# Eight more weight slices decoded by halves, two more chunks turned on VectorE, and a new order for the first 360 steps

## The chip, the cores and the metric

The kernel runs on one core of one Trainium2 chip. The metric is device time in microseconds of one execution. Engines are named as in the profile: PE is TensorE (PEld its weight loads), DVE is VectorE, ACT is ScalarE, POOL is GpSimd, SP is SyncE, which only issues transfers here. A transfer is called a DMA.

## The reference

A gated linear attention recurrence, whose output is the input of a two-layer block with a hard-swish between.

```python
# q, k, v, alpha: (batch 4, heads 8, seq 768, dim 48), float32
state = zeros(B, H, D, D)
for t in range(S):
    state = alpha[:, :, t, :, None] * state + einsum('bhd,bhe->bhde', k[:, :, t], v[:, :, t])
    y[:, :, t] = einsum('bhd,bhde->bhe', q[:, :, t], state)
x = y.transpose(0, 2, 1, 3).reshape(3072, 384)
h = x @ w_in                               # (384, 2048), arrives as float64
g = h * clip(h + 3, 0, 6) / 6
out = g @ w_out                            # (2048, 384), arrives as float64
```

## The kernel before

**Attention.** The 768 positions of each of the four sequences are cut into six chunks of 128, so there are 24 chunks, numbered 0 to 23. For a chunk, alpha, k and q have to stand with the head dimension along the partitions. There are two ways to get there. Chunks below `FIRST` are loaded token by token into a ring of three buffers, one DMA for each of a, k and q, and `transposed` turns each by four 128x128 transposes on PE (line 283) into a PSUM bank; ACT copies alpha out of that bank (`place_alpha`, line 312), and the two products of `scaled` (line 341) read PSUM. Chunks from `FIRST` on are loaded by four DMAs of 32 partitions each for a, k and q (line 264) into `quads`, of which there are two sets used in turn, and DVE turns each by one 32x32-block transpose (line 287 for alpha, line 291 for k and q); `scaled` then reads SBUF (line 343), and POOL clears four columns of the place that alpha was in (line 347). Two running products along the tokens (`decay` line 321, `growth` line 333) give the factors by which k and q are scaled. PE computes scores in two halves of 64 tokens (line 360), the outputs (line 470) and the update of the state (line 444). ACT places q and the state beside scores and v (lines 380 and 433), and copies the finished chunk of x out of PSUM (`keep_x`, line 479) and, for chunks below 8, the turned-back k (`keep_k`, line 392).

**Weights.** The weights come as float64 and are decoded on the chip. They are cut into 16 slices of 128x768 values, 768 KB each, 0 to 7 of `w_in` and 8 to 15 of `w_out`, loaded through five raw buffers (line 161 and line 165). A slice is decoded in five or fewer steps:

- `d1`, `round_low` (ACT, line 185): the low words are scaled and rounded.
- `dx`, `sign` (ACT, line 190): the upper 16 bits of the rounded low words are set from the sign, only for slices in `BY_HALVES`.
- `d2`, `magnitude` (ACT, line 195): the absolute value of the high words.
- `d3`, `high_bits` (DVE): for slices in `BY_HALVES` a clip and a shift (lines 202 and 204), for the others a clip, a shift with a mask, and a third operation that joins the sign (lines 206, 207, 209).
- `d4`, `add_low` (POOL, line 216): the sum of both words as integers.

Before the change slices 0, 1, 2 and 4 go by halves.

**The two layers.** Group g is a pair of chunks. Groups 0 and 1 are done plainly (`ff1` lines 493 and 504, the gate lines 509 and 513, `ff2` line 531). From group 2 on the first layer is done by products of sums of blocks (`product1`, line 617, with sums on DVE), and from group 1 on the second (`product`, line 720).

**Order.** The order is written out by hand as one long string of steps, such as `d3.9` or `tq.4.0`, which are run one after another; each engine does its own instructions in that order, and waits on semaphores for the others. In the string `la`, `lk`, `lq`, `lv` and `w` are loads, and they stand in one queue of SP. `ta`, `tk`, `tq` turn, `ca` is `place_alpha`, `r` and `p` are the running products, `k` and `q` the scalings, `sc`, `u`, `ya`, `yb` the matmuls of the attention, `cy` is `keep_x`. `z.m.n` is filler: matmuls of the identity on n blocks of 128 columns, whose result nobody reads (line 548); 48 of the 49 blocks stand near the start.

## Time and profile before

| | |
|---|---|
| median of 3 runs | 531.0 us (530.9 to 531.11) |
| profiled execution, its own time | 530.91 us |
| its span | 529.1 us |
| mean granted TensorE clock | 0.999 |
| instructions | 15082 |
| DMA bytes read from HBM | 44.50 MB |

The span is what the views of the profile divide; 1.8 us of the profiled execution's time lie outside it. Busy time of an engine is the time in which at least one of its instructions runs. In the strip of 40 slices one slice is 13.2 us. A wait is shown with who ended it.

### The profile page before, as it was taken

Reading aid. Unit: us, or ns where it says so; the run is one execution under the profiler, and the core shown is the slowest. Engines: PE = TensorE matmul, PEld = TensorE weight load, DVE = VectorE, ACT = ScalarE, POOL = GpSimd, SP = SyncE. Lnnn points to the kernel's source line nnn. Section 1 sums busy time; section 2 is a strip of 40 time slices with the busy share of each in tenths; the row PEclk is TensorE's granted clock in tenths of the full one; section 3 lists DMA queues with packets and bytes.
Section 4 is the critical chain, followed back from the end, with each engine's and each line's share of the span. In section 5 each row is a group of like instructions: output and inputs, shape, how many; then the busy total and the mean of one; then the engine's idle time right before and its main releaser. Section 6 shows DMA issues by size and latency. Waiting matters only on the chain.

```text
span 529.1 us, 15082 instructions
## 1 busy us (share of the span) xinstructions
PE 520.6 (98%) x6290; PEld 494.8 (94%) x6290; DVE 462.0 (87%) x838; ACT 259.6 (49%) x513; POOL 55.3 (10%) x89
## 2 busy tenths in 40 slices
PE   8799999999999999999999999999999999999997
PEld 6598886789999999999999999999999999999997
DVE  6998999999999999999999999899988896395471
ACT  4968875112755453464365355454353552543330
POOL 5333543100000100101000000000000000000000
PEclk9999999999999999999999999999999999999999
DMA  9998794213245365445452546153330214000001
GB/s 180 253 240 261 181 269 117 54 32 93 58 118 118 92 135 135 104 95 150 82 145 63 110 118 160 41 124 79 108 84 25 61 22 100 17 26 7 9 9 37
DMA packets 124100, 54.40 MB, mean 103 GB/s; under 512 B 83328, under 2 KB 116864, under 8 KB 124032
## 3 DMA queue, kind: packets, MB, share of 16 engines
q1 hardware_dynamic: 124032, 53.44, 42.8%
q8 instruction: 49, 0.80, 0.7%
q14 instruction: 19, 0.16, 0.1%
HBM read 44.50 MB, written 8.91 MB: 101 GB/s over the span
## 4 chain that ended last, share of the span: by engine, by line
PE 90%; DVE 4%; SPq 2%; DMA 2%; ACT 1%; issue 1%; POOL 0%; DVEq 0%; POOLq 0%; ACTq 0%
PE m_ps L720 36%; PE m_ps L617 31%; PE m_ps L493 6%; PE m_ps L531 4%; PE t_ps L470 4%; PE t_ps L360 2%; PE m_ps L504 2%; PE m_ps L548 2%; PE t_ps L444 1%; PE t_ps L283 1%; DMA rings<-in_alpha_dram 1%; DVE g_sb L554 1%; SPq L253 1%; PE t_ps L388 1%; SPq L410 0%
## 5 line engine op out<-in xcount | busy, mean ns | idle before, releaser
L720 PE MATMUL m_ps<-w,g_sb 128*128 128x192 f32 x704 | 121.8, 327 | 0.0
L623 ACT COPY g_sb<-m_ps 128x512 f32<-128x512 f32 x110 | 63.5, 583 | 116.6 <-PE m_ps L617 91.6
L720 PEld LDWEIGHTS m_ps<-w,g_sb 128*128 128x128 f32 x704 | 113.8, 190 | 0.5
L720 PE MATMUL m_ps<-rings,g_sb 128*128 128x192 f32 x528 | 91.3, 326 | 0.0
L720 PEld LDWEIGHTS m_ps<-rings,g_sb 128*128 128x128 f32 x528 | 85.4, 190 | 0.3
L617 PE MATMUL m_ps<-xc,w 128*128 128x128 f32 x640 | 82.1, 276 | 0.3 <-ACT g_sb L623 0.3
L617 PEld LDWEIGHTS m_ps<-xc,w 128*128 128x128 f32 x640 | 77.7, 192 | 1.2 <-ACT g_sb L623 0.4
L509 ACT ACTIVATE r<-g_sb,half 128x512 f32<-128x512 f32 x80 | 56.8, 721 | 36.3 <-DVE g_sb L558 17.5
L513 DVE SCALAR_TENSOR_TENSOR g_sb<-r,g_sb 128x512 f32<-128x512 f32 x80 | 53.8, 684 | 9.1 <-ACT r L509 8.7
L617 PE MATMUL m_ps<-xT,raw 128*128 128x128 f32 x400 | 53.2, 278 | 0.0
L617 PEld LDWEIGHTS m_ps<-xT,raw 128*128 128x128 f32 x400 | 48.8, 192 | 0.7 <-ACT g_sb L623 0.2
L664 DVE TENSOR_TENSOR g_sb<-g_sb 128x512 f32<-128x512 f32 (+1 forms) x55 | 42.2, 796 | 4.8 <-PE m_ps L720 4.5
L617 PE MATMUL m_ps<-xT,w 128*128 128x128 f32 x320 | 41.8, 277 | 0.0
L617 PEld LDWEIGHTS m_ps<-xT,w 128*128 128x128 f32 x320 | 39.0, 192 | 0.4
L380 ACT COPY A<-q 48x256 f32<-48x256 f32 x88 | 35.4, 402 | 2.9 <-PE t_ps L470 0.8
L370 DVE TENSOR_TENSOR A<-t_ps,mask 64x256 f32<-64x256 f32 x96 | 36.1, 415 | 0.4
L493 PE MATMUL m_ps<-xT,w 128*128 128x256 f32 x144 | 32.5, 381 | 0.0
L617 PE MATMUL m_ps<-xc,raw 128*128 128x128 f32 x240 | 31.9, 276 | 0.0
L321 DVE TENSOR_TENSOR_SCAN R<-t,ones 128x516 f32<-128x516 f32 x24 | 29.5, 1228 | 2.7 <-ACT t L312 2.7
L423 POOL TENSOR_TENSOR st<-sm,R 128x192 f32<-128x192 f32 x20 | 14.7, 737 | 157.2 <-DVE sm L454 157.1
L554 DVE TENSOR_TENSOR g_sb<-g_sb 128x512 f32<-128x512 f32 x40 | 26.9, 679 | 4.1 <-ACT g_sb L623 4.1
L554 DVE TENSOR_TENSOR g_sb<-m_ps,g_sb 128x512 f32<-128x512 f32 x30 | 20.5, 683 | 11.4 <-PE m_ps L617 7.0
(107 smaller groups left out, 718.2 us busy)
## 6 DMA issues: line engine op xcount, KB each, us to landing
raw<-in_moe_w_out_dram SPq DMA_DIRECT2D x8, 768.0 KB, 5.6
raw<-in_moe_w_in_dram SPq DMA_DIRECT2D x6, 768.0 KB, 6.8
v<-in_v_dram SPq DMA_DIRECT2D x48, 96.0 KB, 3.2
out_dram<-oh SPq DMA_DIRECT2D x44, 96.0 KB, 1.7
far<-kq SPq DMA_DIRECT2D x64, 64.0 KB, 2.2
kb<-far SPq DMA_DIRECT2D x64, 64.0 KB, 2.0
aq<-in_alpha_dram SPq DMA_DIRECT2D x36, 96.0 KB, 2.5
kq<-in_k_dram SPq DMA_DIRECT2D x36, 96.0 KB, 2.7
```

What stands on the lines that cost most here:

```text
L321: nc.vector.tensor_tensor_scan(out=reverse(R, n - 1, n), data0=reverse(ax, n, n), data1=reverse(ones, n, n), initial=0.0, op0=ALU.mult, op ...
L370: nc.vector.tensor_tensor(out=to[:, a], in0=sc[a][half], in1=mask[half, half].unsqueeze(1).to_broadcast([HB, NP, HB]), op=ALU.mult)
L380: nc.scalar.copy(out=to[:, a], in_=Q_t[j][64 * a : 64 * a + D, :, half])
L470: nc.tensor.matmul(y_of(j, (i + 1) // 2, p)[:, HB * b : HB * b + HB], vb[:, p, e : e + 32], A_t[j][:, b, 2 * p + a], start=(b == 0 and i = ...
L493: nc.tensor.matmul(h[:, f], w1[:, kk, o : o + C], xT_t[g][:, kk], start=(kk == 0), stop=(kk == KT - 1))
L509: nc.scalar.activation(out=to, in_=h, func=AF.Relu, bias=half, scale=1.0 / 6.0)
L513: nc.vector.scalar_tensor_tensor(out=to, in0=r, scalar=1.0, in1=h, op0=ALU.min, op1=ALU.mult)
L554: eng.tensor_tensor(out=out, in0=in0, in1=in1, op=ALU.add if s1 > 0 else ALU.subtract)
L617: nc.tensor.matmul(acc[g][i][:, f * C : (f + 1) * C], spots[w][:, f * C : (f + 1) * C], x_of(g, x), start=(first and f == 0), stop=last, s ...
L623: nc.scalar.copy(out=slots[z], in_=acc[g][i])
L664: nc.vector.tensor_tensor(out=out, in0=in0, in1=in1, op=ALU.subtract)
L720: nc.tensor.matmul(to[g], a, rhs[:, f], start=(first and f == 0), stop=(last and f == HF - 1), skip_group_check=True)
```

## The change

`BY_HALVES` grows from four slices to twelve: slice 3 and all eight of `w_out` come in, slice 4 goes out. `FIRST` falls from 6 to 4, so chunks 4 and 5 are loaded in quarters and turned by DVE. The first 424 steps of the string become 430 in another order (two steps `ta` fewer, eight `dx` more); from there on the string is the same. The filler keeps its 49 blocks.

```diff
-    BY_HALVES = {0, 1, 2, 4}
+    BY_HALVES = {0, 1, 2, 3, 8, 9, 10, 11, 12, 13, 14, 15}
...
-    FIRST = 6
+    FIRST = 4
...
-        run("""la.1 z.0.2 z.0.5 ta.1.2 la.0 ca.1 lq.1 z.0.2 ta.0.3 z.0.2 w.0 r.1 p.1 tq.1.2 z.0.2
-               la.2 z.0.2 ca.0 r.0 z.0.2 lk.0 z.0.8 q.1 d1.0 p.0 lq.0 dx.0 ta.2.0 z.0.2 lv.0.0 d2.0
...
+        run("""z.0.2 z.0.2 z.0.2 w.1 la.0 z.0.2 la.1 z.0.3 lk.0 d2.1 ta.0.0 z.0.3 ca.0 lq.0 w.0
+               z.0.2 z.0.5 tk.0.2 z.0.2 la.2 d3.1 tq.0.1 d1.1 dx.1 ta.1.3 r.0 p.0 d4.1 k.0 kb.0.2
+               q.0 z.0.2 ca.1 ck.0 z.0.2 r.1 lv.0.0 lk.1 ta.2.1 d2.0 d3.0 d1.0 sv.0.0 dx.0 u.0.2.0
+               sc.0.2.0 z.0.2 sm.0.0 tk.1.3 sv.0.1 m.0 w.2 ca.2 z.0.2 qa.0.1 k.1 d1.2 d2.2 lq.1 la.3
+               ya.0.3 yb.0 cy.0 dx.2 d4.0 sm.0.1 w.3 lq.2 tq.1.1 z.0.8 z.0.2 st.1 ta.3.0 lv.1.1 p.1
...
```

More of the change, by code (lines that the diff above doesn't have):

```diff
@@ L771 @@
     with tc.manual_schedule():
-        run("""la.1 z.0.2 z.0.5 ta.1.2 la.0 ca.1 lq.1 z.0.2 ta.0.3 z.0.2 w.0 r.1 p.1 tq.1.2 z.0.2
-               la.2 z.0.2 ca.0 r.0 z.0.2 lk.0 z.0.8 q.1 d1.0 p.0 lq.0 dx.0 ta.2.0 z.0.2 lv.0.0 d2.0
-               tk.0.1 z.0.2 k.0 lk.1 w.1 tq.0.2 ca.2 kb.0.1 z.0.2 w.2 q.0 ck.0 r.2 qa.0.1 lq.2
-               sc.0.0.2 z.0.2 z.0.2 la.3 qa.1.0 z.0.3 qa.1.1 m.0 p.2 lk.2 u.0.1.3 tk.1.0 lv.1.1
-               z.0.2 w.3 d2.1 d1.1 sm.0.0 k.1 sv.0.1 dx.1 la.4 kb.1.1 z.0.1 ck.1 sm.0.1 sv.0.0
-               tq.2.3 d3.0 d1.2 sc.1.2.1 d4.0 d3.1 lk.3 st.1 z.0.3 dx.2 q.2 m.1 d2.2 z.0.2 tk.2.3
-               ta.3.0 k.2 ca.3 d3.2 u.1.2.1 sv.1.0 r.3 lq.3 sm.1.0 sm.1.1 ya.0.3 yb.0 cy.0 ta.4.0
-               d4.1 fa.0.1 sv.1.1 ca.4 fa.1.2 sc.2.2.1 p.3 d2.3 d4.2 d3.3 ya.1.0 yb.1 w.5 d1.3 m.2
-               fa.2.0 tk.3.3 lv.3.0 d4.3 k.3 w.6 cy.1 lk.4 st.2 fb.2 kb.2.2 kb.3.1 r.4 lv.2.2 d2.5
-               d1.5 fr.0.2.0 fb.1 ck.2 tq.3.0 qa.2.0 d3.5 tk.4.3 d1.6 k.4 q.3 f.0.3.3 ck.3 sv.2.0
-               d2.6 sc.3.2.1 u.2.0.1 u.3.2.3 qa.3.1 fr.0.3.1 d4.5 w.7 fg.0.2 lq.4 d3.6 f.0.5.0
-               sm.2.0 d2.7 w.8 fg.0.3 d1.7 sv.2.1 kb.4.0 d4.6 ck.4 sm.2.1 st.3 d2.8 la.5 d3.7 sv.3.0
-               qa.3.0 sm.3.0 w.9 f.0.6.3 qa.2.1 lk.5 d4.7 sv.3.1 tq.4.0 fb.0 m.3 sm.3.1 fr.0.1.0
-               ta.5.1 p.4 fg.0.1 d3.8 w.4 fr.0.5.1 ca.5 fg.0.5 fr.0.0.0 d1.8 ya.2.2 yb.2 w.10 d4.8
-               cy.2 fg.0.0 lq.5 ya.3.3 yb.3 cy.3 d2.9 la.6 f.0.7.2 lv.4.1 d1.9 d3.9 f.1.7.0 d4.9 r.5
-               fr.0.7.0 d1.4 fr.0.6.1 dx.4 d1.10 w.12 q.4 fg.0.7 p.5 fg.0.6 d2.4 f.1.1.1 d2.10 d3.4
-               tq.5.2 fr.1.7.1 tk.5.1 fr.1.1.0 la.7 f.1.0.2 d2.12 k.5 f.1.3.3 lv.5.0 ca.6 w.11 d4.4
-               fg.1.7 lk.6 fg.1.1 fr.1.3.1 d3.10 d1.12 q.5 f.1.6.0 fr.1.0.0 fg.1.3 fg.1.0 qa.0.0
-               d3.12 d4.10 lk.7 qa.5.0 ca.7 f.1.2.1 d2.11 kb.5.3 st.4 fr.1.6.1 tk.6 ck.5 f.1.4.2
-               w.13 qa.4.0 fg.1.6 d1.11 sc.5.1.0 sc.4.3.2 u.4.3.0 u.5.1 d4.12 fa.4.3 d3.11 d4.11 m.4
-               fr.1.4.1 fr.1.2.0 f.1.5.0 fb.4 w.15 lq.6 sm.4.0 fg.1.2 b.0.0.1 fg.1.4 d2.13 d1.13
-               sv.4.1 r.6 d3.13 w.14 fr.0.4.0 b.1.0.2 k.6 sm.4.1 d2.15 sv.4.0 fg.0.4 tq.6 b.0.1
-               fr.1.5.1 d1.15 b.1.1 d3.15 p.6 d4.13 st.5 fg.1.5 qa.4.1 tk.7 d2.14 s.1.1.1 s.1.0.0
-               d1.14 d3.14 d4.15 qa.5.1 m.5 kb.6.3 b.0.2 d4.14 P.1.0.0 sm.5.0 s.1.3.2 s.1.2.3
-               P.1.1.3 y.1 q.6 lk.8 x.0 x.1 K.1.0 lk.9 y.5 y.0 y.3 sv.5.0 x.2 sv.5.1 b.0.3 s.1.5
-               ck.6 b.1.2 y.2 y.6 r.7 b.1.3 lv.6.2 y.9 G.1.0.0 P.1.2 k.7 K.1.1 y.8 y.10 y.7 y.11
-               la.8 s.1.4 y.4 ya.4.1 yb.4 bo.1 cy.4 xc.2.0 ya.5.0 yb.5 cy.5 xc.2.1 y.16 sc.6.3.2
-               u.6.1.2 P.1.3.3 K.1.2 xc.2.3 y.12 P.1.4 xc.2.4 y.15 x.3 so.1 lv.7.0 G.1.1.1 y.13
-               P.1.5 bo.0 y.17 xc.2.5 y.19 P.1.6 xc.2.7 G.1.2.2 y.20 xc.2.6 y.18 O.1.2 y.21 M.2.0.2
-               y.23 M.2.15.3 n.2.0.8 xc.2.2 M.2.1 xc.2.8 n.2.1.9 la.9 M.2.16 ca.8 sm.6.0 sv.6.1
-               G.1.3.3 xc.2.9 sm.6.1 tk.8 p.7 m.6 r.8 la.10 kb.7.1 M.2.2 M.2.7.0 y.14 lq.7 n.2.2.10
-               M.2.3 M.2.4 lq.8 n.2.7.11 M.2.8 n.2.4.12 p.8 ck.7 z.1.3 st.7 o.2.0.0 M.2.18.1 e.2.0.0
@@ new lines @@
+        run("""z.0.2 z.0.2 z.0.2 w.1 la.0 z.0.2 la.1 z.0.3 lk.0 d2.1 ta.0.0 z.0.3 ca.0 lq.0 w.0
[3 more added lines that the diff above has]
+               ya.0.3 yb.0 cy.0 dx.2 d4.0 sm.0.1 w.3 lq.2 tq.1.1 z.0.8 z.0.2 st.1 ta.3.0 lv.1.1 p.1
+               r.2 ca.3 d1.3 kb.1.3 lk.3 q.1 lk.2 fa.0.1 tq.2.2 d3.2 ck.1 sc.1.1.3 u.1.1.3 d2.3 p.2
+               qa.1.0 q.2 r.3 sm.1.0 z.0.1 d4.2 w.5 fa.2.0 d3.3 lq.3 dx.3 tk.3.0 k.3 fa.1.2 kb.3.2
+               qa.1.1 sv.1.1 d4.3 tk.2.0 sv.1.0 ck.3 m.1 ya.1.1 yb.1 d2.5 cy.1 k.2 d3.5 p.3 w.7 w.6
+               kb.2.2 tq.3.0 qa.2.1 lv.3.0 qa.2.0 d1.5 d2.7 fb.2 sm.1.1 lv.2.2 fb.0 fr.0.2.0 d4.5
+               fb.1 d1.7 w.8 q.3 fg.0.2 ck.2 d2.6 d3.7 f.0.3.3 st.2 la.4 qa.3.0 d3.6 fr.0.1.0 d1.6
+               fg.0.1 fr.0.3.1 sc.3.2.1 sc.2.3.0 u.2.2.0 d4.6 qa.3.1 sm.2.0 d2.8 w.4 u.3.3.1 sv.2.0
+               fr.0.0.0 f.0.5.0 fg.0.3 f.0.6.3 d1.8 sm.2.1 m.3 ca.4 d3.8 st.3 sv.2.1 d4.7 f.0.7.2
+               lk.5 sv.3.0 dx.8 sm.3.0 fr.0.5.1 m.2 w.9 fg.0.0 fg.0.5 r.4 sv.3.1 la.5 ya.2.3 ya.3.2
+               yb.3 yb.2 fr.0.7.0 fr.0.6.1 fg.0.6 p.4 cy.3 cy.2 d2.4 d2.9 d3.4 w.10 lq.4 d1.9 z.0.2
+               d3.9 z.0.2 dx.9 d1.4 f.1.1.1 d1.10 sm.3.1 d4.8 d4.9 f.1.3.3 d4.4 lv.6.2 st.4 ca.5
+               fg.0.7 d2.10 fr.1.1.0 tq.4 fg.1.1 lk.4 f.1.7.0 w.12 r.5 fr.1.7.1 dx.10 f.1.0.2 lq.5
+               fg.1.7 fr.1.0.0 f.1.2.1 w.11 q.4 lv.5.0 fg.1.0 f.1.6.0 d1.12 d2.12 dx.12 tk.4 k.4
+               tk.5 k.5 d2.11 kb.5.1 p.5 d3.12 kb.4.2 fr.1.3.1 f.1.4.2 fg.1.3 ck.5 fr.1.6.1 d1.11
+               tq.5 fa.4.3 la.6 dx.11 lk.6 d4.12 fg.1.6 q.5 d3.10 ck.4 d3.11 fr.1.4.1 ca.6 lv.4.1
+               fr.1.2.0 fg.1.4 fb.4 w.15 d1.15 d2.15 sc.5.1.2 sc.4.0.3 u.5.1 fg.1.2 dx.15 u.4.0.3
+               f.1.5.0 b.0.0.1 d4.11 sv.4.0 w.14 b.1.0.2 m.4 sm.4.0 d4.10 sv.4.1 qa.5.1 qa.4.1 d3.15
+               d4.15 tk.6 sm.4.1 m.5 b.0.1 fr.1.5.1 d1.14 w.13 st.5 d2.14 dx.14 qa.4.0 r.6 lk.7 y.6
+               qa.5.0 k.6 d1.13 fr.0.4.0 kb.6.0 lq.6 ck.6 p.6 b.1.1 y.5 qa.0.0 s.1.1.1 d3.14 sm.5.0
+               tq.6 d2.13 sv.5.0 d4.14 fg.1.5 q.6 dx.13 P.1.0.0 y.1 d3.13 sc.6.3.0 sv.5.1 u.6.3.0
+               ya.4.1 yb.4 ya.5.2 K.1.0 y.10 la.7 fg.0.4 ca.7 d4.13 y.3 x.0 x.1 yb.5 b.1.2 P.1.1.3
+               y.2 s.1.3.2 s.1.0.0 cy.5 b.0.2 y.8 y.7 b.1.3 tk.7 s.1.2.3 lk.8 lk.9 y.0 x.2 b.0.3
+               s.1.5 r.7 y.9 G.1.0.0 P.1.2 k.7 K.1.1 y.11 la.8 s.1.4 y.4 bo.1 cy.4 xc.2.0 xc.2.1
+               y.16 P.1.3.3 K.1.2 xc.2.3 y.12 P.1.4 xc.2.4 y.15 x.3 so.1 lv.7.0 G.1.1.1 y.13 P.1.5
+               bo.0 y.17 xc.2.5 y.19 P.1.6 xc.2.7 G.1.2.2 y.20 xc.2.6 y.18 O.1.2 y.21 M.2.0.2 y.23
+               M.2.15.3 n.2.0.8 xc.2.2 M.2.1 xc.2.8 n.2.1.9 kb.7.1 la.9 M.2.16 ca.8 sm.6.0 sv.6.1
+               G.1.3.3 xc.2.9 sm.6.1 tk.8 p.7 m.6 r.8 la.10 M.2.2 M.2.7.0 y.14 lq.7 n.2.2.10 M.2.3
+               M.2.4 lq.8 n.2.7.11 M.2.8 n.2.4.12 p.8 ck.7 z.1.3 st.7 o.2.0.0 M.2.18.1 e.2.0.0
```

## The prediction

> **What bounds the kernel now.** I read the busy lines and the strip first, then what PE waits for, then busy time by stretch, and last the rows of the operations that the change touches.

> ```profile
> PE 520.6 (98%) x6290; PEld 494.8 (94%) x6290; DVE 462.0 (87%) x838; ACT 259.6 (49%) x513; POOL 55.3 (10%) x89
> ...
> PE   8799999999999999999999999999999999999997
> ...
> DVE  6998999999999999999999999899988896395471
> ACT  4968875112755453464365355454353552543330
> ```

> PE is busy 520.6 of 529.1 us, so the kernel is as long as PE's work plus the little that PE waits. The strip says where another engine is near its limit too: DVE nearly everywhere in the first half, ACT in the first seven slices (0 to 93 us). PE's waits:

> ```profile
> PE t_ps L283 <- DMA rings<-in_q_dram: 1.5, 1, 1.5
> PE m_ps L548 <- POOL ident masks.py:199: 1.5, 1, 1.5
> PE t_ps L388 <- DVE k L341: 1.0, 1, 1.0
> PE t_ps L283 <- DMA rings<-in_alpha_dram: 0.8, 1, 0.8
> PE t_ps L470 <- DVE s L454: 0.4, 1, 0.4
> PE m_ps L617 <- ACT g_sb L623: 0.3, 1, 0.3
> ```

> All but the last fall before 28.5 us (5.4 us with a 0.2 not shown): the start is bound by loads and by DVE. From then on PE runs without a gap to 130 us, while DVE and ACT look like this:

> ```profile
> core 0: us, PE busy (x) PEld busy (x) DVE busy (x) ACT busy (x) POOL busy (x), PEclk, DMA share, GB/s
> 10.00:90.00 80.00, 76.39 (x994) 64.05 (x993) 76.50 (x123) 64.61 (x105) 31.14 (x30) 1.00 0.93 222
> 90.00:110.00 20.00, 20.00 (x86) 14.52 (x85) 19.82 (x31) 2.20 (x6) 2.34 (x5) 1.00 0.19 47
> ```

> Between 10 and 90 us ACT has 15.4 us free, DVE 3.5, and the DMA engines are busy 0.93 of the time. From 90 to 110 us ACT is nearly idle. The step string is the same again from about the turning back of chunk 7's k (line 388 at 128.70 us in the chain), so whatever happens happens before; after it PE carries a lead or a lag unchanged to the end.

> **The operations touched**, from the timeline and the groups by form:

> ```profile
> 61.00 1.04 PE L283 MATMUL t_ps<-ident,rings 128*128 128x128 f32 x8
> L190 ACT ACTIVATE raw<-raw 128x768 f16<-128x768 int32 x3 | 5.8, 1938 | 0.1
> L209 DVE SCALAR_TENSOR_TENSOR raw<-raw,w 128x768 uint32<-128x768 uint32 x11 | 10.8, 978 | 0.4
> L287 DVE STREAM_TRANSPOSE t<-aq 128x512 f32<-128x512 f32 x18 | 19.8, 1110 | 0.3 <-POOL t L347 0.3
> L291 DVE STREAM_TRANSPOSE kt<-kq 128x512 f32<-128x512 f32 x18 | 12.7, 704 | 0.0
> L312 ACT COPY t<-t_ps 128x512 f32<-128x512 f32 x6 | 3.5, 583 | 2.6 <-PE t_ps L283 2.6
> ```

> **PE: 2.6 us of work gone.** Six steps (a, k and q of chunks 4 and 5) of four transposes leave: 24 matmuls. The eight of the row at 61.00 hold PE 0.87 us in the chain (61.16 to 62.04), 0.109 each, so 24 are 2.6 us. Filler (49 blocks), scores, updates, outputs and both layers keep their counts. PE had no gap after 28.5 us, so this shortens the kernel one for one if everything else keeps up.

> **DVE: 2.7 us less.** Eight slices lose line 209 (0.96 us in most of its rows): 7.7 us. The clip and shift stay: lines 206 and 207 on a `w_out` slice take 0.55 and 0.56, and lines 202 and 204 differ only in their constants; a gain or loss of 0.13 each would be the contiguous against the strided slice (0.69 in the `w_in` rows), in sum 0 taken, at most 2.1 us. Two transposes of line 287 (1.11) and four of line 291 (0.70) come in: 5.0 us. The two scalings of a chunk cost 0.68 from PSUM (line 341) and 0.68 from SBUF (line 343): nothing. So DVE, which is the tightest engine after PE, gives back as much as PE does. That is why PE's saving can be passed on at all: with DVE unchanged at 76.5 of 80 us, PE would soon wait for it.

> **ACT: 14.4 us more.** Eight signs at 1.94 are 15.5; two alpha copies at 0.58 go, 1.2. No row shows a sign on a `w_out` slice; the nearest are the four on `w_in` slices, 1.93 to 2.00, and raw words are read and written with the same stride, so I take 1.94. From 10 to 90 us ACT would then be busy 64.6 + 14.4 = 79.0 of 80 us. Here lies the risk. [...]

> ACT's own waits before 100 us are partly for landed slices (rows of 3.7, 1.2 and 0.8 us for lines 195 and 185, 5.7 in sum), the rest mostly for PE and DVE, and those shrink by themselves when ACT runs late. PE needs four things from ACT: x (`cy`), k turned back (`ck`), the placed state (`sv`) and the placed q; behind a sign in ACT's queue they come up to 1.94 late. In the new order I find signs one or two steps ahead of such steps about five times between 50 and 95 us. PE stands in runs of line 493 of 8 to 10 us there, which hide most of it: I count 0.2 for each, +1.0 us, with ends 0 (all hidden) and 2.0 (one whole sign shown).

> **SP and DMA.** Six loads of one DMA each become 24 quarters: 18 issues more at about 0.45 us (SP's rows of line 264), 8 us of SP's queue, and the quarters' landings lie 0.43 us apart in the trace at 71 to 75 us, 1.7 a load, against 1.0 to 1.3 between whole loads at 3.8 to 6.1 us: 0.5 us longer each, 3.0 us of DMA time. Behind them in SP's queue stand the `w_out` slices and v. In before SP waits there for POOL to free raw buffers (from 56.5 to 61.0, for instance), so part of this time was waiting anyway: I take it as hidden, with ends 0 and 3.0. POOL has two 0.1 us memsets more and the same sums; its own 1.47 to 2.65 us per slice stay.

> **The start: 0, from -1.0 to +0.7.** The new string puts slice 1 ahead of all else in SP's queue. A slice alone takes 5.4 us from issue to landing (40.88 to 46.29), so alpha of chunk 0 lands near 7.3 instead of 3.8 us; the filler ahead of it (11 blocks instead of 7) lasts to 6.4, a wait of 1.0. Chunk 2's alpha lands behind two slices and four loads, near 14.5: 1.1. Then 0.8 for v of chunk 0, 1.2 for its outputs behind DVE's masks, 0.5 in small ones; with the 1.5 until the identity is there, 6.1 us against 5.4. Laid out in the same way the old order comes to 7.1, 1.7 more than was measured; less that, the new one would be 4.4. I take no change. In return slice 1 is decoded 10 us earlier.

> **Sum.** -2.6 (PE) + 1.0 (behind ACT) + 0 + 0 = -1.6 us. The profiled execution took 530.9 us (span 529.1 and 1.8 around it), 0.1 below the median of 531.0: 529.4 us.

> **Rivals.**
> - *The saving arrives whole* (528.4): the runs of line 493 hide every late copy. For it: PE did not wait once from 28.5 to 130 us in before. Against: ACT at 79 of 80. [...] 0.20.
> - *Late loads give it back* (531.0 - 2.6 + 3.0 = 531.4): all 3.0 us of longer loads reach PE as late slices. For: the DMA share of 0.93. Against: SP's waits for POOL. 0.12.
> - *ACT becomes the bound* (slower): if its 5.7 us of waits for landings stay, it needs 79.0 + 5.7 = 84.7 us for what it did in 80, is 4.7 late at 90 us, and PE waits for x, k and state by as much: 531.0 - 2.6 + 4.7 = 533.1. It decides from 2.6 us on. Against: overflow into 90 to 110 us, where ACT has 17.8 us free. 0.17.
> - *The late start stays* (slower): all 3.5 us by which the first alpha comes later pass through, 531.0 - 2.6 + 1.0 + 3.5 = 532.9. Against: the filler only moves, and PE has the same work to do. 0.07.
> - That the change does nothing can be left out: in the built program's order line 283 falls from 72 to 48 matmuls, line 209 from 12 to 4, line 190 rises from 4 to 12.

> **Numbers.** The forecast keeps 0.44, of which 0.06 lies within 0.2% (1.1 us, about what a measurement of this kernel can tell from no change). Faster: 0.38 + 0.20 = 0.58. Same: 0.06 + 0.12 = 0.18. Slower: 0.17 + 0.07 = 0.24. Range: below, the whole saving and the best start, 531.0 - 2.6 - 1.0 = 527.4; above, ACT's rival, 533.1.

> **What would show it.** PE busy near 518 us; DVE near 459; ACT near 274, with 9s in slices two to seven. PE's waits after 28.5 us should name ACT lines 479, 392 or 433, and sum to about 1 us; waits before it to about 5.4. ACT idle of several us between 30 and 90 with PE still waiting for it would mean that slices came late, not that ACT was full. Wrong altogether: signs on `w_out` slices far from 1.94, or PE waiting for POOL's sums (line 216).

## The result, and the profile after

The changed kernel takes 534.0 us (median of 22 runs, 530.01 to 537.65) against 530.9 us for the kernel before (22 runs, 530.47 to 532.93): ratio 1.0061, 95% interval 1.004 to 1.0081. It is slower by some 3 us, or 0.6%; that is little, but the interval does not reach 1. The forecast was 529.4, faster, and 534.0 lies above its range.

The profiled execution took 535.85 us, span 534.1, mean granted clock 0.993. The busy lines and the strips of the page of after:

```profile
PE 520.1 (97%) x6266; PEld 494.1 (93%) x6266; DVE 459.5 (86%) x836; ACT 273.0 (51%) x519; POOL 57.6 (11%) x91
...
PE   7799899999999999999999999999999999999997
PEclk9999799999999999999999999999999999999999
...
DVE  6899679999999999999999999898997896395471
ACT  5998579602654564363455355444354552543330
```

DVE (459 forecast) and ACT (274) are as busy as the prediction had them. What was not there before is a hole in all strips in the fifth slice (53 to 67 us), with the clock down to 0.7 in the same slice. The waits of PE in after:

```profile
PE t_ps L470 <- issue: 3.9, 1, 3.9
PE t_ps L283 <- DMA rings<-in_alpha_dram: 2.0, 2, 1.4
PE m_ps L548 <- POOL ident masks.py:199: 1.5, 1, 1.5
PE t_ps L470 <- DVE k L341: 1.2, 1, 1.2
PE t_ps L283 <- DMA rings<-in_q_dram: 0.7, 1, 0.7
...
PE m_ps L617 <- ACT g_sb L623: 0.3, 1, 0.3
```

The first line is new, and it names no engine: "issue" is time in which PE waited for nothing that the profile shows. None but the last is a wait for ACT, and that one was there before. The timeline of PE around it (start, length, idle before in brackets):

```profile
50.18 1.99 PE L470 MATMUL t_ps<-A,v 128*32 128x64 f32 x124
56.05 0.43 PE L470 MATMUL t_ps<-A,v 128*32 128x64 f32 x4 [3.88 <-issue]
56.41 2.08 PE L548 MATMUL m_ps<-ident 128*128 128x256 f32 x4
```

PE stops in the middle of one run of equal instructions: the outputs of chunks 2 and 3 (`ya` and `yb`, line 470) are 128 matmul records; 124 run, then nothing for 3.88 us, then the last four. These read the same kinds of tiles as the 124 ahead of them, so a missing tile is no likely reason to split the run there. Busy time by stretch in after:

```profile
core 0: us, PE busy (x) PEld busy (x) DVE busy (x) ACT busy (x) POOL busy (x), PEclk, DMA share, GB/s
10.00:90.00 80.00, 72.84 (x962) 62.11 (x961) 68.70 (x115) 67.22 (x99) 32.55 (x34) 0.96 0.89 218
90.00:110.00 20.00, 20.00 (x264) 14.77 (x263) 19.25 (x27) 12.59 (x20) 3.83 (x3) 1.00 0.38 79
...
50.00:60.00 10.00, 6.12 (x139) 4.89 (x138) 6.70 (x9) 5.68 (x11) 1.58 (x1) 0.77 0.88 196
```

ACT was not full from 10 to 90 us (67.2 of 80, where 79.0 were forecast): its work slid into 90 to 110 us, 12.6 us where before had 2.2, without making PE wait. The clock is at half from 55.48 to 62.31 us, 6.83 us, twice the 3.41 us that such a stretch lasts in e8 below. PE stands still in the first 0.57 us of that; in the rest the matmuls of line 493 begin 0.427 us apart in the median, against 0.216 at full clock. So the half clock costs half of the other 6.26 us, 3.1 us of PE's work.

**Where the 5.0 us between the two profiled spans lie** (534.1 - 529.1). PE idle: 14.0 us against 8.55, of which +3.9 is the gap, +1.0 the start (waits up to 40 us 6.1 against 5.1), +0.3 between 130 and 160 us, +0.2 at the end. PE busy: 520.1 against 520.55, of which -2.6 is the 24 transposes, +3.1 the slow clock, and -1.0 a clock that is full from 4.28 us on instead of 6.36 (in before six fillers take 3.35 us ahead of that, two take 0.60 behind it). Without the gap and the slow clock the span would be 534.1 - 3.9 - 3.1 = 527.1, 2.0 less than before.

**The timed runs go with the clock.** Half of 3.41 us is 0.0032 of 534 us, so by an estimate a mean clock of 0.997 stands for one stretch of 3.41 us at half clock, 0.993 for two and 0.990 for three; of the profiles e8 has 0.997 with one, after and e7 have 0.993 with two. Of the 22 runs of after, 3 have 0.999 or 1.0 and take 530.0 to 531.2 us; 11 have 0.996 or 0.997, 532.6 to 535.4; 8 have 0.993 or 0.990, 534.7 to 537.65. Such a stretch need not follow the gap, nor cost much: in the profiles of e7 and e12 below one begins at 16.4 us, and of 80 runs of the kernel before that were timed beside the experiments, the 28 with 0.997 take 531.2 us in the median, the 39 with 1.0 take 530.9. So that the gap with a stretch at half clock behind it is the loss in the other runs of after too is likely, but only two profiles of that kernel (after and e7) show it.

### The profile page after: what moved, and what is told of

It reads as the page before. It is cut to its first block, busy times and chain, and to the rows that moved or that the text cites. A ratio compares the mean times of both kernels' runs of the same rounds, so it can differ in the third digit from the quotient of the medians.

```text
span 534.1 us, 15053 instructions
## 1 busy us (share of the span) xinstructions
PE 520.1 (97%) x6266; PEld 494.1 (93%) x6266; DVE 459.5 (86%) x836; ACT 273.0 (51%) x519; POOL 57.6 (11%) x91
## 3 DMA queue, kind: packets, MB, share of 16 engines
HBM read 45.48 MB, written 8.91 MB: 102 GB/s over the span
## 4 chain that ended last, share of the span: by engine, by line
PE 72%; DVE 11%; DMA 6%; ACT 4%; SPq 3%; issue 2%; POOL 1%; DVEq 0%; POOLq 0%; ACTq 0%
PE m_ps L720 32%; PE m_ps L617 30%; PE t_ps L470 3%; PE m_ps L493 2%; PE t_ps L360 2%; DMA v<-in_v_dram 2%; DMA rings<-in_q_dram 1%; PE t_ps L444 1%; PE m_ps L504 1%; DVE g_sb L554 1%; DMA rings<-in_alpha_dram 1%; SPq L253 1%; SPq L161 1%; ACT A L380 1%; DVE rings L664 1%
## 5 line engine op out<-in xcount | busy, mean ns | idle before, releaser
L623 ACT COPY g_sb<-m_ps 128x512 f32<-128x512 f32 x110 | 63.5, 583 | 116.6 <-PE m_ps L617 91.6
L617 PE MATMUL m_ps<-xc,w 128*128 128x128 f32 x640 | 82.2, 276 | 0.6 <-DVE g_sb L554 0.3
L617 PEld LDWEIGHTS m_ps<-xc,w 128*128 128x128 f32 x640 | 77.7, 192 | 1.6 <-DVE g_sb L554 0.5
L617 PE MATMUL m_ps<-xT,raw 128*128 128x128 f32 x400 | 53.0, 278 | 0.0
L617 PEld LDWEIGHTS m_ps<-xT,raw 128*128 128x128 f32 x400 | 48.7, 192 | 0.7 <-ACT g_sb L623 0.2
L617 PE MATMUL m_ps<-xT,w 128*128 128x128 f32 x320 | 41.8, 277 | 0.0
L617 PEld LDWEIGHTS m_ps<-xT,w 128*128 128x128 f32 x320 | 39.0, 192 | 0.4
L493 PE MATMUL m_ps<-xT,w 128*128 128x256 f32 x144 | 34.1, 397 | 0.0
L493 PEld LDWEIGHTS m_ps<-xT,w 128*128 128x128 f32 x144 | 28.6, 201 | 4.3
L617 PE MATMUL m_ps<-xc,raw 128*128 128x128 f32 x240 | 31.9, 276 | 0.0
L321 DVE TENSOR_TENSOR_SCAN R<-t,ones 128x516 f32<-128x516 f32 x24 | 30.9, 1286 | 0.0
```

Of the source, the lines that this page charges most:

```text
L321: nc.vector.tensor_tensor_scan(out=reverse(R, n - 1, n), data0=reverse(ax, n, n), data1=reverse(ones, n, n), initial=0.0, op0=ALU.mult, op ...
L493: nc.tensor.matmul(h[:, f], w1[:, kk, o : o + C], xT_t[g][:, kk], start=(kk == 0), stop=(kk == KT - 1))
L617: nc.tensor.matmul(acc[g][i][:, f * C : (f + 1) * C], spots[w][:, f * C : (f + 1) * C], x_of(g, x), start=(first and f == 0), stop=last, s ...
L623: nc.scalar.copy(out=slots[z], in_=acc[g][i])
```

## The experiments

**The theory (A in the expectations): PE's own code came late.** The profile has a queue of its own for instructions. The row of after (before has the same, with 0.7%):

```profile
q8 instruction: 49, 0.80, 0.6%
```

That is 49 packets, 0.80 MB, 16 KB each. PE has 6266 matmul and 6266 weight load records, 12,532 together, and 0.80 MB over these is 64 bytes each; a packet is then 256 instructions. The queue grows with PE's records: e9 and e10 below, with 208 more, have 50 packets, and e11, with 512 more, has 51. I counted PE's records in the trace in order of time, from 0, with the 81 semaphore and drain instructions of its queue. The gap is ahead of record 1473. Block edges that fit all the gaps lie at 193 + 256 n: 449, 705, 961, 1217, 1473, and so on. The packet that moves while PE stands still is the fifth of the queue (number 4, counted from 0): in after it moves from 53.46 to 54.66 us, and PE goes on at 56.05.

Two things decide then: when PE passes the edge before (1217), and how long the packet stands behind data in the DMA engines. That a packet goes with the edge before its own block is read from the traces: the first 48 packets of before and of after moved from 3.5 us ahead of PE's passing that edge to 4.7 us behind it, while PE took 2.0 to 30.5 us from there to the next edge. The outputs, scores and updates are many very small matmuls (line 470: 124 in 1.99 us), so a block there lasts only 2.7 us (e3) to 3.0 us (after) behind the edge before, where the 256-wide matmuls of line 493 (27 in 5.99 us at full clock, in e13) would last an estimated 28 us. After the experiments the table is this (times in us from the traces; the share is the DMA share of the windows view from 44 to 48 us, over 1 where packets overlap in the records):

| run | DMA share, 44 to 48 | edge 1217 passed | packet 4 moves | record 1473 ready to go | it goes |
|---|---|---|---|---|---|
| before | 0.74 | 48.86 | 47.95 to 48.89 | 52.66 | 52.66 |
| e3, loads later | 0.90 | 49.43 | 48.98 to 50.04 | 52.1 | 52.1 |
| e8, the same again | 1.00 | 49.08 | 52.21 to 53.47 | 52.0 | 54.93 |
| after | 1.09 | 49.22 | 53.46 to 54.66 | 52.2 | 56.05 |
| e7, the same again | 1.09 | 49.06 | 53.00 to 54.59 | 52.0 | 56.11 |
| e2, 16 records more | 1.11 | 46.92 | 50.89 to 52.21 | 51.7 | 53.76 |
| e1, 104 more | 1.09 | 43.19 | 47.98 to 49.45 | 52.5 | 52.5 |
| e13, 48 more | 1.10 | 44.31 | 48.57 to 49.65 | 51.6 | 51.6 |
| e12, 104 more | 1.09 | 42.48 | 46.54 to 48.00 | 51.8 | 51.8 |

In the last three rows the packet is as late behind the edge as in after, 4.1 to 4.8 us, but the block lasts 7.3 to 9.3 us, since the edges fall earlier in the work; so PE doesn't stop.

All 18 profiles together bear this out. PE has 23 waits on issue of over 0.2 us in them, none in before, and each stands at one of these edges to within one record. Of 868 blocks PE began none sooner than 1.26 us after its packet had landed. And the crowd shows: of the 441 packets with a DMA share below 0.5 in the 4 us ahead of them none moved more than 2.3 us behind its edge, while the 100 with a share above 1 moved 3.2 us behind in the median.

The rivals: the gap belongs to its place in the work (the burst of line 470, or what it reads, under heavy loading); a part of the change (turning on DVE, or signs on ACT) costs the time; or the later loads do. In the expectations the letters of the rivals are local to each text.

### Moving the block edges

**e1 and e2** cut early filler blocks into single matmuls (46 of the 49 blocks stand early, the other three far behind). Filler does nothing but keep PE busy; cut, it has more instructions for the same work, so all later edges fall earlier in the work.

```diff
-  z.0.2          # e1: all 18 early steps, 46 blocks; e2: the fourth to seventh z.0.2 only
+  z.0.1 z.0.1
```

Expected of e1: 

> The changed kernel with its 46 early filler blocks cut into one matmul each: the same filler time, 26 matmuls (104 PE instructions) more ahead of the 3.9 us gap that PE has at 52 us. Theory A (PE has run out of instructions: a 16 KB block of its code, 256 instructions, was asked for when the last but one was used up, near 47 us, and came at 54.7): the edge of the block moves 104 instructions up, into the matmuls near 42 us, so the code is there before the burst; the gap at the end of the four attention outputs goes, the clock stays full, time 528 to 530 us. A smaller gap can come up at another edge. Theory B (PE waits there for data, of ScalarE, VectorE or a load): the gap stays at the same matmul, 533 to 536 us.

Measured: 532.37 us (531.53 to 537.62, 10 runs), 1.0031 [1.0008, 1.0055]. The time is above theory A's 528 to 530. In the profile of e1 there is no stop at record 1473, the clock is 1.0, the span 530.3. Instead there is a new stop, of 1.6 us, four blocks earlier, at record 449 = 1473 - 4 x 256:

```profile
22.11 0.44 PE L283 MATMUL t_ps<-ident,rings 128*128 128x128 f32 x2 [1.60 <-issue]
```

Expected of e2: 

> The changed kernel with four of its two-block fillers cut in single blocks: 4 matmuls, 16 PE instructions, more in the first 25 us, no time. Theory A (code): the gap stays between the same two places of the code, so it comes 16 instructions earlier in the program: 8 matmul records earlier, 116 records of the outputs ahead of it and 12 behind instead of 124 and 4; time about as the changed kernel, 531 to 536. Theory B (data): the gap stays ahead of the last four records.

Measured: 531.91 us (530.47 to 534.64, 10 runs), 1.0015 [0.9996, 1.0035]. The stop moved within the same run of matmuls: it now stands ahead of the last twelve records, and it lasts 2.09 us, with the clock staying full.

```profile
53.76 0.42 PE L470 MATMUL t_ps<-A,v 128*32 128x64 f32 x12 [2.09 <-issue]
```

Both moved the stop to where the count of instructions said. The 16 records of e2 are 8 matmul and 8 weight load records, and the split moved by just 8 matmul records, from 4 to 12 ahead of the end of the run.

**e11** adds instructions in another place: 128 small matmuls just ahead of `tq.2.2`, each in two passes, 512 records, two whole blocks. (256 records were meant; a matmul turned out to be two passes, each with its weight load.)

```diff
+    def little(n):
+        for _ in range(n):
+            nc.tensor.matmul(bank_m[0][0:32, 0:64], ident[:, 0:32], ident[:, 0:64],
+                             start=True, stop=True)
...
-  fa.0.1 tq.2.2
+  fa.0.1 u0.128 tq.2.2
```

Expected: 

> As e9 with 128 of the small matmuls: 256 records, one whole block, so that every later edge falls on the same place in the work as in the changed kernel. Theory A: the gap is back at the same place (3 to 5 us, ahead of the last 4 matmuls of line 470), and the fillers cost 128 x 0.017 - 0.67 = 1.5 us: span 535 to 536, time 535 to 537. Theory C (any filler at 25 us helps, by delaying PE against the loads): no gap, like e9 and 1.3 us slower than it, time near 530.

Measured: 546.83 us, 1.0293 [1.0277, 1.031], most of it the added work (256 passes in 14.48 us, less what PE would have waited there). The timeline of e11 (lines behind 550 stand 6 further down there):

```profile
63.93 1.99 PE L470 MATMUL t_ps<-A,v 128*32 128x64 f32 x124
68.75 0.30 PE L470 MATMUL t_ps<-A,v 128*32 128x64 f32 x4 [2.82 <-issue]
```

With whole blocks added, PE stops ahead of the same last four matmuls, 12.7 us later in time and at record 1985 = 1473 + 512. e1 and e2 moved the stop by moving the count; here the time moved by 12.7 us and the count by whole blocks, and the stop kept its place in the work. So the count of instructions sets the place, and neither the time nor the burst by itself; and filler does not help by merely delaying PE, since no kernel delays it more than this one.

**e9** has 52 of the same matmuls (208 records, no whole block).

```diff
-  fa.0.1 tq.2.2
+  fa.0.1 u0.52 tq.2.2
```

Expected: 

> The changed kernel with 52 very small matmuls more (128x32 by 128x64, 0.017 us each by the row of line 470) just ahead of the turning of q of chunk 2, where PE waits 0.67 us at 25 us for q: 104 instruction records more. Theory A (PE's own code comes in blocks of 256 instructions and came late at record 1473): from there on every block edge falls 104 records earlier in the work, so the block that was late is asked for at about 41 us and needed at about 51 us; no wait on issue at 52 us, the clock stays full, and the fillers cost 0.9 - 0.67 = 0.2 us. Span 534.1 - 3.9 - 3.4 + 0.2 = 527.0, time near 528.8, faster than before (531.0). Theory B (the gap belongs to this place in the order: the burst of small matmuls, or what they read, under the heavy loading): the gap of 3.9 us stays right behind the burst, span 534 to 534.5, time near 534.5.

Measured: 538.92 us (537.11 to 539.09, 4 runs), 1.014 [1.0126, 1.0153]. The price was wrong: they took 5.99 us instead of 0.9, since a pass cost 0.058 and not 0.017, and there were twice as many. Clock 1.0 in the profile, and the stop of 3.9 us is gone, but four smaller ones (1.2, 1.0, 0.6 and 0.5 us, all put down to issue) at other edges take 3.3 us together.

**e12 and e13** let the small matmuls write the four quarters of the bank in turn, as line 470 does: 26 of them (104 records) and 12 of them (48).

```diff
-            nc.tensor.matmul(bank_m[0][0:32, 0:64], ident[:, 0:32], ...
+            nc.tensor.matmul(bank_m[0][32 * (a % 4) : 32 * (a % 4) + 32, 0:64], ident[:, 0:32], ...
```

Expected of e12: 

> As e9, but with 26 of the small matmuls, which write the four quarters of the bank in turn as line 470 does, so that a pass should cost 0.017 us as there (in e9 104 passes in one quarter took 5.99 us): 104 instruction records, 26 x 2 x 0.017 = 0.9 us less the 0.67 us that PE waits there. Theory A (code blocks): the edge that was late is asked for some 6 us earlier; no wait on issue above 1 us, the clock stays full, span 527 to 528.7, time 528.8 to 530.5, just faster than before. Theory D (whatever is moved, some other edge or another engine takes the room): waits on issue or on VectorE of 2 us or more elsewhere before 80 us, time 531 to 534.

Expected of e13: 

> As e12 with 12 of them: 48 records, 0.4 us, inside the wait of 0.67 us for q. Theory A: the block is asked for about 3 us earlier than in the changed kernel and needed at about 51.6 us, so the gap is 0 to 1.5 us and too short to cost clock; time 528.6 to 531. Theory D: time 531 to 534.

Measured: e12 531.39 us (530.58 to 532.73, 12 runs), 1.0007 [0.9998, 1.0017]; e13 531.49 us (529.57 to 532.19, 12 runs), 0.9999 [0.9987, 1.0012]. Work was added and nothing else changed, and the kernel became 2.5 us faster in the median than the changed one (534.0), equal to the one before; theory A's times, up to 530.5 and 531, were missed by less than 1 us. The spread of runs fell from 7.6 us (22 runs) to 2.1 and 2.6 (12 runs each). In the profile of e13 (span 527.8, clock 1.0) PE is busy 518.9 us, where the prediction had about 518 and the fillers take 0.5 more, and the stops are small:

```profile
44.31 5.99 PE L493 MATMUL m_ps<-xT,w 128*128 128x256 f32 x27 [0.24 <-issue]
97.06 0.31 PE L470 MATMUL t_ps<-A,v 128*32 128x64 f32 x5 [0.67 <-issue]
```

**e15 and e16** are e13 again, one execution each, for the profile.

Expected of e15: 

> e13 a second time, for its profile: its times were 529.57 to 532.19, and the profiled run was the fastest of them. Theory A alone: the slower runs have a wait on issue at another edge between 40 and 100 us, 0.5 to 2.5 us. Theory D: they have longer waits for VectorE, ScalarE or loads.

Expected of e16: 

> e13 a third time, for the profile of one more execution. Theory A alone: a run near 532 has a wait on issue of 0.5 to 2.5 us at another edge of the code. Theory D: it has longer waits for VectorE, ScalarE or loads.

Measured: 531.24 us (span 529.5) and 530.09 us (span 528.3), clock 1.0. PE's waits in e15, which is close to the median of e13:

```profile
PE t_ps L470 <- issue: 0.9, 1, 0.9
PE t_ps L360 <- ACT kb L392: 0.7, 1, 0.7
...
PE m_ps L493 <- issue: 0.5, 1, 0.5
```

PE is busy 518.8 of 529.5 us, so idle 10.7, against 8.55 in before: the two stops for code (0.9 at 98 us, 0.5 at 44 us) and one late k placed by ACT (0.7) are 2.1 of it. So the 1.7 us of PE work that e13 has less than before is spent again, two thirds of it on code at other edges, one third on ACT, and both theories of the expectation hold in part. e16 has 1.0 and 0.4 us for code at the same two edges, and no late k.

The stop at 97 to 101 us, at record 2497, is in the profiles of e1 and e12 to e16, 0.7 to 1.4 us long. No crowd stands there. The stretch of e13 just ahead of its stop:

```profile
94.00:98.00 4.00, 3.33 (x151) 2.66 (x141) 4.00 (x5) 2.58 (x5) 1.84 (x1) 1.00 0.01 4
```

The last two numbers are the DMA share, 0.01, and GB/s; in the six profiles the share of these 4 us is at most 0.14. PE used up the block ahead in 2.1 to 2.5 us, and from its first record to PE's going on took 3.1 to 3.6 us. So a burst can outrun its code with idle DMA engines too; with full ones the stops were longer, up to 5.0 us. In e1 and e12 the view of waits puts this stop down to copies of ACT (lines 699 and 705), but these had ended 0.7 and 0.9 us before PE went on, and the packet had landed 1.4 and 1.5 us before, as at the other stops.

### Fewer data in front of the code

**e3 and e8** issue k and a of chunk 5 later, by 25 and 14 steps, just behind weight slice 10; q of chunk 4, which stood there, follows them (e8 is e3 again, one execution).

```diff
-  ... f.0.7.2 lk.5 sv.3.0 ... sv.3.1 la.5 ya.2.3 ... w.10 lq.4 d1.9
+  ... f.0.7.2 sv.3.0 ... sv.3.1 ya.2.3 ... w.10 la.5 lk.5 lq.4 d1.9
```

Expected of e3: 

> The changed kernel with alpha and k of chunk 5 loaded behind weight slice 10 instead of ahead of it (ten DMAs later in SP's queue). Near 47 us fewer data packets then stand in the DMA engines. Theory A with its cause in the data queue: the code block is asked for at the same instruction but comes 2 to 4 us earlier, the gap at 52 us shrinks to under 2 us or goes, the clock stays full, 528.5 to 531.5 (a later alpha of chunk 5 may cost some). Theory A with a fixed time for a block: gap and time as before. Theory B: no smaller gap unless the wait was for a load behind these two.

Expected of e8: 

> The kernel with alpha and k of chunk 5 loaded behind slice 10, unaltered: its profiled run took 530.2 us with no gap, its other runs 532 to 535. Theory A: in a slower run a block of code is late again at one of the edges (instruction 1217 or 1473), because it stands behind data in the DMA engines by chance; the waits for ScalarE (0.7 us) stay as they are. Otherwise: the same waits, longer, for ScalarE or VectorE, and no gap without a semaphore.

Measured: e3 532.98 us (530.15 to 535.02, 10 runs), 1.0039 [1.0022, 1.0056]; e8 533.19. The two profiles of this one kernel are the best evidence for what holds the packet up, since the code is the same. In e3 the DMA share from 44 to 48 us is 0.90, the packet moves at 48.98, there is no stop, the clock is 1.0 and the span 528.4. In e8 the share is 1.00, the packet moves at 52.21, and:

```profile
54.93 0.43 PE L470 MATMUL t_ps<-A,v 128*32 128x64 f32 x4 [2.90 <-issue]
```

The clock is at half for 3.41 us behind it. With the rows of before, after, e2 and e7 in the table, the packet moved 0.9 us ahead of the edge up to 4.2 us behind it, on the whole the later the fuller the DMA engines were from 44 to 48 us. That it stands behind data is read from these cases and from the count over all profiles; the trace doesn't have the moment at which the packet is asked for. A stop for one that came late was 0.2 to 5.0 us here.

**e14** has the fillers of e13 and the order of loads of e3 together.

Expected: 

> e13 (12 small matmuls, 48 records) with the three loads of e3 issued behind weight slice 10. Theory A: no code gap at 52 us, and less data in front of the code fetches, so the runs lie closer together than those of e13; the shift and the smaller crowd add up if both only serve the fetch: time 529.3 to 530.8, faster than before. Theory D (the rest of the change's saving is lost to late data or late VectorE work that the shift does not touch): 531 to 533, as e3 and e13.

Measured: 532.75 us (530.5 to 534.81, 11 runs), 1.003 [1.0014, 1.0045], slower than e13. Theory A's forecast fell: the two do not add up. Its profile (span 532.0, clock 1.0) has stops for code of 1.2 and 0.9 us and waits of 1.4 for DVE (line 513) and 0.7 for ACT. A wait for line 513 of over 1 us is in both profiles that have small matmuls and the later loads (e14 and e10), and in none that has the small matmuls alone; how the later loads lead to it was not traced.

**e10**, with the 52 fillers of e9 and those loads, shows the same beside the price of the fillers.

Expected: 

> As e9, with the loads of a and k of chunk 5 and q of chunk 4 issued behind the load of weight slice 10, as in e3. Theory A: as e9, no gap and full clock, span 527 to 528, time 528.5 to 529.5; with the smaller crowd in the DMA engines the runs lie closer together than in e9. Theory B: the gap is between that of e3 and of the changed kernel, 0 to 3.9 us, and the time 530 to 534, spread as in e3.

Measured: 537.85 us (536.58 to 541.1, 5 runs), 1.0129 [1.011, 1.0148]; PE waits 2.6 us for the gate of line 513 at 80 us, and 1.6 and 0.9 us for code. Both theories had 0.2 us for the fillers, so neither number could come out.

### The parts of the change alone

**e4** is the kernel before with `FIRST = 4` only: the chunks 4 and 5 are loaded in quarters and turned by DVE, in the old order.

```diff
-    FIRST = 6
+    FIRST = 4
...
-  ta.4.0
-  ta.5.1
```

Expected: 

> The kernel of before with FIRST = 4 alone (its order with the two PE turns of alpha of chunks 4 and 5 left out; decoding as before). PE loses the same 2.6 us, VectorE gains 5.0 us of transposes and loses nothing. If VectorE's relief by the halves was needed: VectorE, full between 52 and 116 us, passes part of its 5 us on to PE, 530 to 534 us. If PE's saving stands alone: 528.5 us. Theory A adds: PE's code is shifted by 16 to 24 instructions at 52 us; if a gap comes without a semaphore it is at a multiple of 256 instructions.

Measured: 541.14 us (539.39 to 541.53, 4 runs), 1.0171 [1.0141, 1.0202]. This is far above both forecasts. DVE is at 468.0 us busy (462.0 before), and PE waits for it and for code, with three stretches of 3.41 us at half clock (mean clock 0.991). The longer stop for code is at record 1473:

```profile
PE t_ps L470 <- issue: 4.6, 2, 3.9
PE t_ps L360 <- DVE q L341: 2.6, 1, 2.6
```

**e5** is the kernel before with the new `BY_HALVES` only, each added sign right behind its rounding.

```diff
-    BY_HALVES = {0, 1, 2, 4}
+    BY_HALVES = {0, 1, 2, 3, 8, 9, 10, 11, 12, 13, 14, 15}
...
-  d1.3           # likewise 8 to 15; dx.4 goes
+  d1.3 dx.3
```

Expected: 

> The kernel of before with the new BY_HALVES alone: in the old order each new sign stands right behind its d1, slice 4 loses its sign; turns of chunks 4 and 5 stay on PE. PE's code is that of before, so theory A (code) expects no gap without a semaphore. VectorE loses 7.7 us, ScalarE gains 15.5 and is at about 80 of 80 us between 10 and 90. If ScalarE bounds, PE waits for lines 479, 392, 380 or 433, several us in sum, 533 to 538 us; if the runs of line 493 hide it, 531 us as before.

Measured: 536.28 us (534.72 to 536.65, 4 runs), 1.0083 [1.0054, 1.0111]. No stop for code, as PE's code is that of before. DVE is busy 457.5 us, 4.5 less, and still PE waits for it:

```profile
PE m_ps L493 <- DVE g_sb L513: 2.0, 1, 2.0
```

The longer wait ends at 70.78 us. The timelines of ACT and of DVE ahead of it:

```profile
63.54 1.93 ACT L190 ACTIVATE raw<-raw 128x768 f16<-128x768 int32 x1
65.21 0.94 ACT L195 ACTIVATE w<-g_sb 128x768 f32<-128x768 f32 x1
```

```profile
66.19 0.69 DVE L206 TENSOR_SCALAR w<-w 128x768 f32<-128x768 f32 x1 [1.64 <-ACT w L195]
```

An added sign stands ahead of the magnitude of another slice (line 195) in ACT's queue, DVE waits 1.64 us for that, and the gate behind it on DVE (line 513) comes too late for PE. With 1.1 us of waiting for ACT's copy of x (line 479), 0.5 more at the start and one stretch of 3.41 us at half clock behind the longer wait (1.7 us) this makes up 5.3 of the 5.5 us of span. Here ACT does hold PE up, much in the way of the prediction's third rival.

**e6** is the changed kernel with the old `BY_HALVES`, in the new order.

```diff
-    BY_HALVES = {0, 1, 2, 3, 8, 9, 10, 11, 12, 13, 14, 15}
+    BY_HALVES = {0, 1, 2, 4}
...
-  dx.3           # likewise 8 to 15
...
-  d1.4
+  d1.4 dx.4
```

Expected: 

> The changed kernel with the old BY_HALVES (its new order, signs of slices 3 and 8 to 15 left out, one for slice 4 put behind its d1). PE's code is that of the changed kernel instruction for instruction, VectorE has 7.7 us more, ScalarE 13.6 less. Theory A (code): if PE comes to the burst of outputs at the same time, the gap stands again ahead of the 1474th PE instruction, whatever ScalarE does. Theory B (a wait for ScalarE): with ScalarE relieved the gap goes. Beside it VectorE, full again, costs PE some us later: 533 to 540 us in sum.

Measured: 542.24 us (538.82 to 544.39, 4 runs), 1.0197 [1.015, 1.0244], DVE busy 465.4. The same stop, longer, and DVE late:

```profile
PE t_ps L470 <- issue: 5.0, 1, 5.0
PE m_ps L720 <- DVE g_sb L513: 2.7, 1, 2.7
```

So without the halves DVE is late (e4, e6), and the halves in the old order, placed right behind the rounding, make ACT late (e5). The stop goes with the third part, `FIRST = 4`: e4 has it in the old order, e6 without the added halves, and before and e5, with `FIRST = 6`, don't have it. The new order is not needed for it, and no run has that order with `FIRST = 6`. With `FIRST = 4` each of six loads reads 352 KB in four quarters (two of 96 and two of 80 KB) instead of 192 KB in one, and what the kernel reads from HBM rises from 44.50 to 45.48 MB. In e4 the DMA share is 1.08 from 52 to 56 us, ahead of its stop; in e6 it is 1.09 from 44 to 48. PE also has 48 records fewer, which shifts the edges. Which of the two decides was not tried.

**e7** is the changed kernel a second time, for its profile.

Expected: 

> The changed kernel, unaltered: a second profile. [...] Theory B: the gap moves with the data.

Measured: 534.42 us, span 532.6. The stop is at the same record, of about the same length, with one stretch of 3.41 us at half clock behind it (another begins at 16.4 us):

```profile
56.11 0.31 PE L470 MATMUL t_ps<-A,v 128*32 128x64 f32 x4 [4.10 <-issue]
```

## Why the prediction was wrong, point by point

**The step that failed** is the sentence under PE: "PE had no gap after 28.5 us, so this shortens the kernel one for one if everything else keeps up." The list of what has to keep up had DVE, ACT, SP's queue, the loads and POOL; PE's own code was not on it. Two rows that I had read bore on it: the DMA share of 0.93 from 10 to 90 us, and, in the page, the instruction queue with its 49 packets, 0.7% of the time of those same 16 DMA engines. The price of the missing term was 3.9 us of stop and 3.1 us of clock in the profiled run; in the second profile of the same kernel (e7) it was 4.1 us and one stretch at half clock, 1.7 us. Without it the profiled span would have been 2.0 us below before, where the sum had 1.6, so the rest of the sum held to 0.4 us. None of the four rivals had it, and the two slower ones (ACT as the bound, a late start) are not what happened, although ACT's 533.1 is near the result.

**The terms of the sum.**
- PE, -2.6: nearly right. In e13, at full clock, PE is busy 518.9 us with 0.5 of filler in it, so 518.4 against 520.6 before, 2.2 less, and the prediction had about 518.
- DVE, 2.7 less: 2.5 measured (459.5 against 462.0).
- ACT, 14.4 more: 13.4 measured; signs on `w_out` slices take 1.93, as taken from the `w_in` rows. The row by form of after:

```profile
L190 ACT ACTIVATE raw<-raw 128x768 f16<-128x768 int32 x11 | 21.3, 1933 | 0.2
```

- Copies behind ACT, +1.0: too large for after, which has no new wait for ACT (the 0.3 at line 617 was there before); 0.7 us appears in each of e3, e14 and e15, so its bounds held. What was wrong was that ACT must do it all by 90 us: it did 12.6 us between 90 and 110.
- SP and DMA, 0 of 0 to 3.0: no slice came late to PE, as I took it. But the term had only one victim in mind. The crowd was real, and it held up the code. The term was also sized by landings alone: the 0.98 MB that the quarters read more are an estimated 4.4 us at the 222 GB/s that before has from 10 to 90 us.
- The start, 0: right in sum by luck, from two errors that cancel in the profiled run: the waits before 40 us grew by 1.0 us, and the clock was full 2.08 us earlier, which is worth 1.0.
- The rival that the saving arrives whole would have been 2.6 us less; by the accounting above 2.0 us less in span were left. The fastest run of after, at 530.01, and of e13, at 529.57, come near; the medians don't.

**The clock as a second price.** A wait was costed at its length. In after it cost nearly twice that, 3.9 us of stop and 3.1 us of clock: the half clock began 3.31 us into the stop and lasted 6.83 us. Every stretch at half clock in the profiles is 3.41 us or 6.83, but for those that the end of a trace cuts off. Waits of 1.95 us for DVE in e5 and 2.56 in e10 and a stop of 2.90 in e8 had one behind them, while stops of 2.09 us in e2 and 1.60 in e1 cost no clock. So the length of a wait does not settle by itself whether the clock falls, and what does was not shown.

**What stays open.** The stop at record 1473 was narrowed down to `FIRST = 4`, but the bytes of the quarters, their number and the shifted edges were not tried one by one. When the packet is asked for is not in the trace. And no version was found that is faster than the kernel before beyond the uncertainty: e13 is equal to it.

## What to carry to other kernels

When an engine runs many tiny instructions, count its instructions as a supply too: PE's code came here in 49 packets of 16 KB, 256 instructions each, through the same DMA engines as the data. Bursts that used up a block in 2.1 to 3.0 us stopped it, for 0.7 to 1.4 us with idle DMA engines (a share of at most 0.14) and for up to 5.0 us with full ones (1.09 in e6), with "issue", or an engine that had long been done, as the only name in the waits and a run of equal instructions cut at an odd place. A wait of TensorE has to be priced with the clock that it may cost too: waits of 1.95 us (e5) to 4.10 us (e7) had a stretch of 3.41 us at half clock behind them, worth up to 1.7 us of PE's work, though one of 2.09 us (e2) had none. And where such a stop is suspected, shift the edges by a few dozen cheap instructions: if the stop moves with the count, as in e2 (8 matmul records), and comes back after a whole block, as in e11, it is the code.
